# A gated recurrence and a feed-forward block in one kernel: the instruction order of every engine set by a written time plan

## The chip, the cores and the metric

The kernel runs on one core of a Trainium2 chip. Its engines run side by side, each through its own list of instructions in order: TensorE (PE in the tables, with PEld for its weight loads), VectorE (DVE), ScalarE (ACT), GpSimd (POOL) and SyncE (SP), which here only starts DMAs; ACT can start DMAs too. They wait for each other on semaphores. The metric is the device time of one execution in microseconds, as a median of several runs.

## The reference

The inputs are q, k, v and alpha, each (4 batches, 8 heads, 768 steps, 48), and two weights, w_in (384 x 2048) and w_out (2048 x 384), which arrive as 64-bit floats. For every batch and head a 48 x 48 state runs over the steps; its output, with the heads side by side, is the input x (3072 x 384) of a feed-forward block:

```python
for t in range(S):
    state = alpha[:, :, t, :, None] * state + np.einsum('bhd,bhe->bhde', k[:, :, t], v[:, :, t])
    y[:, :, t] = np.einsum('bhd,bhde->bhe', q[:, :, t], state)
...
h = x @ w_in
g = h - np.tanh(h)
return (g @ w_out).astype(np.float32)
```

## The kernel before, in words

`fast` does the work; `general` is a slower path that runs only if a check of the value ranges fails at the end, which it does not here. The 3072 rows are cut into 12 units of 256 steps (three per batch), each of two chunks of 128 steps.

**Attention of a unit (`gla`).** `load` brings alpha, k and q into the tiles `ar`, `kr`, `qr` (four DMAs each, one copy of each tile) and v into `vt` (two DMAs). DVE turns them with 32 x 32 transposes (L363) into aT, kT and qT. Two scans on DVE run the products of alpha backwards (U, L369) and forwards (W, L378); `ends` (L373 to L375) are U's values at chunk borders. POOL multiplies kT by U and qT by W (L383); ACT squares both scans for the range check (L386). Then for each chunk: PE makes the scores kT x qT (`sc`, L401), DVE masks them (`pm`, L404), POOL lets the old state decay (L408), PE adds state x qT (L413) and v x scores (L417) into `y`, and ACT copies `y` into `xT`, the feed-forward's input, and its last heads into `xs` (L423, L424). Six small DMAs, started by ACT, move `xs` into the free rows of xT (L430). For the next chunk PE transposes kT (`tp`, L437), ACT copies it (`kn`, L438), PE multiplies it with v (`up`, L441), and DVE adds that to the state (L446, L448).

**Feed-forward of a unit (`moe`).** Eight slices s of 256 hidden features. `first(s)`: 12 matmuls w_in x xT into a PSUM tile `h` (L461; two such tiles), three squaring passes on ACT and a check pass (L467 to L469, L474), three passes on DVE that end in `g` (L470 to L472). `second(s)`: eight matmuls of g with w_out into the two accumulators `o` (L481). The two alternate, with `second` two slices behind; at the end of a unit two `second`s stand together, and ACT and SP store `o` (L493, L494).

**Weights.** Each of the 8 slices of w_in and of w_out arrives as a 128 x 768 tile `raw` of 8-byte numbers (L41, four such tiles in all) and is rounded to float32 by ACT (two passes, L57 and L58), DVE (three, L60 to L65) and POOL (one add, L68). So unit 0's feed-forward cannot run ahead of its weights; the later units have them.

**What sets the order.** `put` gives every step a number, the steps are emitted in the order of these numbers (L497 to L532), and from the emitted program a scheduler then chooses the order in which each engine executes. Loads are queued on SP in the order which that scheduler found; in unit 0, k and v go by ACT's queue. The code emits v and k of unit 0 and the first weight slices about together; in the trace SP starts with the first slice of w_in.

Of the kernel before, what the change touches and what calls it, by code (L numbers as in the profile page):

```python
# [16 lines left out]
P = 128  # L17
HP = 64
# [26 lines left out]
def round_weight(nc, pool, raw, dst):  # L45
# [3 lines left out]
    V, A, GP = nc.vector, nc.scalar, nc.gpsimd  # L49
    if raw.dtype == FP32:  # L50
        A.copy(dst, raw.rearrange("p (j n) -> p j n", n=dst.shape[-1]))
        return
# [3 lines left out]
    last = pool.tile([P, WN], I32, name="last")  # L56
    A.activation(mag, hi.bitcast(FP32), AF.Abs)  # L57
    A.activation(last, lo, AF.Copy, scale=2.0 ** -29)  # L58

    V.tensor_scalar(out=mag, in0=mag, scalar1=2.0 ** (896 // 8 - 127), scalar2=2.0 ** (1151 // 8 - 127) * 1.875,  # L60
                    op0=ALU.max, op1=ALU.min)
    bits = mag.bitcast(I32)
# [4 lines left out]
    n = dst.shape[-1]  # L67
# [187 lines left out]
def fast(tc, q, k, v, alpha, moe_w_in, moe_w_out, out, w_in, w_out, ident, ok, pad_rows):  # L255
# [17 lines left out]
    with ExitStack() as ctx:  # L273
# [20 lines left out]
        for t, x in zip(raws, (1.0, 0.0, 0.0)):  # L294
            GP.memset(t[:, :, R - 1, :], x)
# [7 lines left out]
        for t in (after, before):  # L303
            GP.memset(t, 0.0)
        GP.memset(after[:, P::P + 1], 1.0)
# [18 lines left out]
        def round_in(s):  # L324
            round_weight(nc, two, raw_in.pop(s), w_in[:, :, 2 * s * P:2 * (s + 1) * P])

        def round_out(s):
            round_weight(nc, two, raw_out.pop(s), w_out[:, 2 * s:2 * s + 2, :])

        loaded = {}  # L330

        def load(u):
            b, i = divmod(u, UPB)
            t0 = i * TU
            for n, (t, x) in enumerate(zip(raws, (alpha, k, q))):
                queue = A if u == 0 and n == 1 else nc.sync
# [8 lines left out]
            vt = loaded[u] = three.tile([P, CU, H, D], FP32, name="vt")  # L345
            for c in range(CU):
                (A if u == 0 else nc.sync).dma_start(out=vt[:, c], in_=v[b, :, t0 + c * P:t0 + (c + 1) * P, :].rearrange("h p d -> p h d"))

        xT = {}

        def gla(u):
# [3 lines left out]
            vt = loaded.pop(u)  # L355
            kT, qT = (two.tile([P, NP, CU, P], FP32, name=n) for n in ("kT", "qT"))
            U, W = (two.tile([P, N, P + 1], FP32, name=n, bufs=1) for n in ("U", "W"))
            U_, W_ = (t.rearrange("p n t -> p (n t)") for t in (U, W))
            aT = aTs[u % 2]
            tail = aT[:, 1:].rearrange("p (n t) -> p n t", t=P + 1)  # L360
            for t, raw in zip((tail[:, :, 0:P].rearrange("p (g c) t -> p g c t", c=CU), kT, qT), raws):
                for g in range(NP):
                    V.transpose(t[:, g].rearrange("p c (i r) -> p r c i", r=R),  # L363
                                raw[:, g, :, 0:32])
                yield
                if t is not kT and t is not qT:


                    V.tensor_tensor_scan(out=U_[:, ::-1], data0=aT[:, :0:-1], data1=after[:, ::-1],  # L369
                                         initial=0.0, op0=ALU.mult, op1=ALU.add)  # L370
                    ends = two.tile([P, NP, CU], FP32, name="ends")
                    e = ends.rearrange("p g c -> p (g c)")
                    V.tensor_reduce(out=least[:, u:u + 1], in_=U[:, :, 0], axis=AX.X, op=ALU.min)  # L373
                    V.tensor_single_scalar(out=e, in_=U[:, :, 0], scalar=1.0 / R_MAX, op=ALU.max)
                    V.reciprocal(before[:, 0::P + 1], e)  # L375
                    yield

                    V.tensor_tensor_scan(out=W_, data0=aT[:, 0:N * (P + 1)], data1=before, initial=0.0,  # L378
                                         op0=ALU.mult, op1=ALU.add)
                    yield  # L380
            for n, (t, x) in enumerate(((kT, U), (qT, W))):
                t = t.rearrange("p g c t -> p (g c) t")
                GP.tensor_mul(t, t, x[:, :, 1:])  # L383
                x = x.rearrange("p n t -> p (n t)")
                junk = two.tile([P, N * (P + 1)], FP32, name="junk", bufs=1)
                A.activation(junk, x, AF.Square,  # L386
                             accum_out=sizes[:, 2 * u + n:2 * u + n + 1])
            yield

            x_t = xT[u] = two.tile([P, KT, TU], FP32, name="xT")  # L390
            xs = two.tile([P, TU], FP32, name="xs")
            for c in range(CU):
# [3 lines left out]
                sc = [ps_sc.tile([P, NP, P], FP32, name=f"sc{hh}") for hh in range(2)]  # L396
                pm = [two.tile([P, NP, P], FP32, name=f"pm{hh}") for hh in range(2)]
                for g in range(NP):
                    for hh in range(2):
                        at = slice(HP * hh, HP * hh + D)  # L400
                        T.matmul(sc[hh][:, g, :], lhsT=kT[at, g, c, :], rhs=qT[at, g, c, :],  # L401
                                 start=True, stop=True)
                for hh in range(2):
                    V.tensor_mul(pm[hh], sc[hh], mask.unsqueeze(1).to_broadcast([P, NP, P]))  # L404
                if n > 0:
                    for hh in range(2):
                        at = (slice(HP * hh, HP * hh + D), slice(None), slice(HP * hh, HP * hh + D))
                        GP.tensor_mul(old[at], old[at], ends[at[0], :, c:c + 1].to_broadcast([D, NP, D]))  # L408
                yield
                y = ps_y.tile([P, NP, P], FP32, name="y", tag="y")  # L410
                if n > 0:
                    for g in range(NP):
                        T.matmul(y[0:EV, g, :], lhsT=old[:, g, :], rhs=qT[:, g, c, :],  # L413
                                 start=(g == 0), stop=False, skip_group_check=True)
                for g in range(NP):
                    for hh in range(2):
                        T.matmul(y[HP * hh:HP * hh + D, g, :], lhsT=vt[:, c, 2 * g + hh, :],  # L417
                                 rhs=pm[hh][:, g, :], start=(n == 0 and g == 0), stop=True,
                                 skip_group_check=True)
                to = slice(c * P, (c + 1) * P)  # L420
                for hh in range(2):
                    at = slice(HP * hh, HP * hh + D)
                    A.copy(xs[at, to], y[at, NP - 1, :])  # L423
                    A.copy(x_t[at, :, to], y[at, 0:KT, :])  # L424
                if c == CU - 1:
                    for hh in range(2):
                        for j in range(KT):
                            at, f0 = pad_rows[j][2 + hh]
                            r0 = HP * hh + f0 - (H - 2 + hh) * D
                            A.dma_start(out=x_t[at, j, :], in_=xs[r0:r0 + at.stop - at.start])  # L430
                yield
                if last:
                    continue
                kn = two.tile([P, NP, P], FP32, name="kn")
                tp = ps_y.tile([P, NP, P], FP32, name="tp", tag="tp")
                for g in range(NP):
                    T.transpose(tp[:, g, :], kT[:, g, c, :], ident)  # L437
# [175 lines left out]
```

## Time and profile before

| What | Value |
|---|---|
| median of three runs | 749.27 us (747.30 to 749.41) |
| profiled execution, its own time | 749.17 us |
| its span, from the first to the last instruction | 745.9 us |
| granted clock of TensorE, mean | 0.961 |
| busy: PE, PEld, DVE, ACT, POOL | 648.4, 470.9, 423.4, 332.7, 117.5 us |
| share of PE's busy time: `h` and `o` groups | 282.2 and 267.2 us |
| DMA: bytes in all | 50.99 MB |
| one weight slice; a unit's alpha, k or q; a unit's v | 768; 736; 384 KB |

A busy share over the whole span mixes the start, where the weights arrive, with the later units, so it is to be read by stretches: a windows view gives each engine's busy time in a stretch, a waits view who stood for whom, a timeline the instructions in order. The sizes come from the table of DMA issues (each transfer of alpha, k and q is cut into four, of 192 and 176 KB, and v into two of 192).

### The profile page before, as it was taken

To read this page: it belongs to the slowest core of one execution; us is meant where nothing else is said; L and a number is where in the kernel's file an instruction comes from. 1 tells how busy PE (TensorE), PEld (TensorE's weight loads), DVE (VectorE), ACT (ScalarE), POOL (GpSimd) and SP (SyncE) were. 2 spreads that over 40 slices of the span, in tenths; PEclk is the share of its full clock that TensorE was granted. 3 is DMA by queue.
4 is the path that set the end of the run, shared out by engine and by line. 5 is a ranking of instruction groups with operands and counts; after the bars stand their busy time and mean duration, and the time that the engine had idled before them with its cause. 6 is when DMAs were issued, how large, how long until landed. Compare 5 with 4: busy or idle time off the path is not lost.

```text
span 745.9 us, 8678 instructions
## 1 busy us (share of the span) xinstructions
PE 648.4 (87%) x3089; PEld 470.9 (63%) x3089; DVE 423.4 (57%) x636; ACT 332.7 (45%) x701; POOL 117.5 (16%) x98
## 2 busy tenths in 40 slices
PE   0367629587999899999999998999999999999996
PEld 0255317455767677776767776777676777777773
DVE  0828662677677676866747636737447253343432
ACT  1135431555256445455544543543554353444542
POOL 2403331333120221110201201202002000000000
PEclk9998965799999999999999999999999999999998
DMA  9615930943036417424512511402200000000000
GB/s 174 169 20 155 229 89 1 206 75 93 8 92 133 98 37 148 98 60 95 119 51 61 119 32 24 84 22 60 49 22 6 21 1 7 22 1 6 21 1 26
DMA packets 57268, 50.99 MB, mean 68 GB/s; under 512 B 29440, under 2 KB 52096, under 8 KB 57216
## 3 DMA queue, kind: packets, MB, share of 16 engines
q1 hardware_dynamic: 52256, 48.02, 28.8%
q10 hardware_dynamic: 4960, 2.33, 1.6%
q8 instruction: 26, 0.43, 0.2%
q14 instruction: 26, 0.21, 0.1%
HBM read 44.43 MB, written 4.72 MB: 66 GB/s over the span
## 4 chain that ended last, share of the span: by engine, by line
PE 70%; DVE 12%; DMA 6%; ACT 4%; issue 3%; POOL 3%; ACTq 1%; SPq 0%; DVEq 0%; POOLq 0%
PE h L461 30%; PE o L481 29%; PE y L417 5%; PE up L441 2%; DVE z L471 2%; PE sc L401 2%; DVE w L470 2%; DVE W L378 2%; ACT u L467 2%; DVE pm L404 1%; DMA kr<-in_k_dram 1%; DMA raw<-in_moe_w_out_dram 1%; PE y L413 1%; PE tp L437 1%; POOL w_in L68 1%
## 5 line engine op out<-in xcount | busy, mean ns | idle before, releaser
L461 PE MATMUL h<-xT,w_in 128*128 128x256 f32 x1152 | 282.2, 391 | 17.3 <-POOL w_in L68 11.9
L481 PE MATMUL o<-w_out,g 128*128 128x384 f32 x768 | 267.2, 496 | 10.5 <-DVE g L472 10.4
L461 PEld LDWEIGHTS h<-xT,w_in 128*128 128x128 f32 x1152 | 217.0, 194 | 63.9 <-POOL w_in L68 14.8
L481 PEld LDWEIGHTS o<-w_out,g 128*128 128x128 f32 x768 | 148.5, 194 | 101.3 <-issue 18.8
L470 DVE TENSOR_TENSOR w<-h,u 128x512 f32<-128x512 f32 x96 | 66.3, 690 | 210.4 <-ACT u L467 209.8
L467 ACT ACTIVATE u<-h 128x512 f32<-128x512 f32 x96 | 57.2, 596 | 181.7 <-PE h L461 150.4
L408 POOL TENSOR_TENSOR state<-state,ends 48x192 f32<-48x192 f32 x40 | 30.5, 762 | 303.7 <-DVE state L448 190.5
L471 DVE SCALAR_TENSOR_TENSOR z<-z,w 128x512 f32<-128x512 f32 x96 | 70.6, 736 | 8.7 <-ACT z L468 0.5
L472 DVE SCALAR_TENSOR_TENSOR g<-z,z 128x512 f32<-128x512 f32 x96 | 68.2, 710 | 7.9 <-ACT z L469 0.4
L468 ACT ACTIVATE z<-u 128x512 f32<-128x512 f32 x96 | 60.6, 631 | 3.0
L469 ACT ACTIVATE z<-u 128x512 f32<-128x512 f32 x96 | 59.0, 615 | 0.0
L474 ACT ACTIVATE big<-u 128x512 f32<-128x512 f32 x96 | 59.0, 615 | 0.0
L423 ACT COPY xs<-y 48x128 f32<-48x128 f32 x48 | 12.5, 260 | 98.6 <-PE y L417 98.3
L437 PE MATMUL tp<-ident,kT 128*128 128x128 f32 x80 | 14.1, 302 | 47.0 <-POOL kT L383 46.0
L417 PE MATMUL y<-pm,vt 128*48 128x128 f32 x384 | 38.1, 298 | 11.7 <-DVE pm L404 11.7
L437 PEld LDWEIGHTS tp<-ident,kT 128*128 128x128 f32 x80 | 10.6, 154 | 53.2 <-POOL kT L383 46.8
L383 POOL TENSOR_TENSOR kT<-kT,U 128x1024 f32<-128x1024 f32 x12 | 27.0, 2250 | 105.6 <-DVE kT L363 86.0
L417 PEld LDWEIGHTS y<-pm,vt 128*48 128x48 f32 x384 | 25.4, 131 | 25.7 <-DVE pm L404 20.7
L404 DVE TENSOR_TENSOR pm<-sc,mask 128x512 f32<-128x512 f32 x48 | 31.7, 684 | 16.3 <-PE sc L401 16.3
L363 DVE STREAM_TRANSPOSE kT<-kr 128x256 f32<-128x256 f32 x48 | 25.7, 622 | 19.2 <-DMA qr<-in_q_dram 17.8
L401 PEld LDWEIGHTS sc<-qT,kT 48*128 48x128 f32 x384 | 29.1, 210 | 11.2 <-issue 9.5
L383 POOL TENSOR_TENSOR qT<-qT,W 128x1024 f32<-128x1024 f32 x12 | 26.2, 2180 | 61.5 <-DVE qT L363 61.5
(56 smaller groups left out, 462.1 us busy)
## 6 DMA issues: line engine op xcount, KB each, us to landing
raw<-in_moe_w_out_dram SPq DMA_DIRECT2D x8, 768.0 KB, 7.2
raw<-in_moe_w_in_dram SPq DMA_DIRECT2D x16, 288.0 KB, 5.5
ar<-in_alpha_dram SPq DMA_DIRECT2D x24, 192.0 KB, 5.0
qr<-in_q_dram SPq DMA_DIRECT2D x24, 192.0 KB, 4.4
out_dram<-ob SPq DMA_DIRECT2D x24, 192.0 KB, 1.9
ar<-in_alpha_dram SPq DMA_DIRECT2D x24, 176.0 KB, 4.2
qr<-in_q_dram SPq DMA_DIRECT2D x24, 176.0 KB, 4.8
kr<-in_k_dram SPq DMA_DIRECT2D x22, 192.0 KB, 4.3
```

The source lines that it names most:

```text
L383: GP.tensor_mul(t, t, x[:, :, 1:])
L401: T.matmul(sc[hh][:, g, :], lhsT=kT[at, g, c, :], rhs=qT[at, g, c, :], start=True, stop=True)
L417: T.matmul(y[HP * hh:HP * hh + D, g, :], lhsT=vt[:, c, 2 * g + hh, :], rhs=pm[hh][:, g, :], start=(n == 0 and g == 0), stop=True, skip_gro ...
L461: T.matmul(h[:, a, :], lhsT=w_in[:, j, f * P:(f + 1) * P], rhs=x_t[:, j, :], start=(j == 0), stop=(j == KT - 1))
L467: A.activation(sq, h, AF.Square)
L468: A.activation(z1, sq, AF.Square, bias=QB1, scale=QA)
L469: A.activation(z2, sq, AF.Square, bias=QB2, scale=QA)
L470: V.tensor_mul(w, h, sq)
L471: V.scalar_tensor_tensor(out=z1, in0=z1, scalar=QK1, in1=w, op0=ALU.add, op1=ALU.mult)
L472: V.scalar_tensor_tensor(out=g, in0=z2, scalar=QK2, in1=z1, op0=ALU.add, op1=ALU.mult)
L474: A.activation(big, sq, AF.Relu, bias=-U_MAX, accum_out=over[:, n:n + 1])
L481: T.matmul(o[c], lhsT=g[:, a * TU + c * P:a * TU + (c + 1) * P], rhs=w_out[:, f, :], start=(f == 0), stop=(f == FT - 1))
```

## The change

The generators `gla` and `moe`, whose steps were spread evenly, are taken apart: every step gets a number of its own from a plan, and the steps are emitted within `tc.manual_schedule()`, under which each engine executes its instructions, and each queue starts its DMAs, in the order of the numbers. What is computed stays the same. In detail:

- The order of loads: unit 0's operands (alpha and q by SP, k and v by ACT), two slices of w_in, one of w_out, one of w_in, unit 1's operands, the moves of xs, then w_out and w_in slices by turns.
- The six moves of `xs` are started by SP (before: ACT).
- The rounding of a weight slice is cut into three steps with numbers at, at+1 (DVE) and at+3 (POOL).
- In unit 0 POOL's products come in halves, one per chunk, and the second chunk's scores use the two `h` tiles of PSUM, not the `sc` tiles.
- `first(s)` is split into its matmuls and `shrink` (ACT and DVE), 2.8 later. In units 1 to 11 `first` comes every 6.6 and `second` 16.5 after its `first`, across the border of units too; a unit's attention stands in the plan 46 before its feed-forward, its loads 8 earlier still.
- `ends` takes its maximum with a tile of constants (a new memset on POOL) in place of a constant. The memsets of the operand tiles' last rows go from POOL to DVE.

```diff
     for t, x in zip(raws, (1.0, 0.0, 0.0)):
-        GP.memset(t[:, :, R - 1, :], x)
+        V.memset(t[:, :, R - 1, :], x)
...
+    def put(at, do, *args):
+        plan.append((at, len(plan), do, args))
+
+    def convert(at, make, s):
+        it = []
+        put(at, lambda: (it.append(make(s)), next(it[0])))
+        put(at + 1, lambda: next(it[0]))
+        put(at + 3, lambda: next(it[0], None))
...
+    def ends():
+        U = m["U"]
+        e = m["ends"] = two.tile([P, NP, CU], FP32, name="ends")
+        e = e.rearrange("p g c -> p (g c)")
+        V.tensor_tensor(out=e, in0=U[:, :, 0], in1=low, op=ALU.max)
...
+    for name, by in (("kT", "U"), ("qT", "W")):
+        if u == 0:
+            for c in range(CU):
+                put(at[name + by] + c, scale, name, by, slice(c, c + 1))
+        else:
+            put(at[name + by], scale, name, by, slice(0, CU))
...
+    def moves():
         for hh in range(2):
...
-                    A.dma_start(out=x_t[at, j, :], in_=xs[r0:r0 + at.stop - at.start])
+                nc.sync.dma_start(out=xT[u][part, j, :], in_=m["xs"][r0:r0 + part.stop - part.start])
+    put(at["moves"], moves)
...
     for s in range(FS):
+        put(first_at[s], first, s)
+        put(first_at[s] + 2.8, shrink, s)
+        put(second_at[s], second, s)
+    put(second_at[-1] + 2.8, store)
...
+    put(0, load, 0)
+    for at, what, s in ((0.1, fetch_in, 0), (0.2, fetch_in, 1), (0.3, fetch_out, 0), (0.4, fetch_in, 2)):
+        put(at, what, s)
+    put(20, load, 1)
+    for s in range(1, FS):
+        put(31 + 6 * s, fetch_out, s)
+        if s + 2 < FS:
+            put(34 + 6 * s, fetch_in, s + 2)
+    gla(0, dict(aT=6, U=8, kT=10.3, ends=12.3, kTU=12.4, W=12.8, qT=15.2, qTW=17.2, sizeU=13.5, sizeW=18,
+                scores=(19.4, 21.4), masked=(21.4, 23.4), decay=(0, 19.5), y=(23.4, 25.4), x=(25.3, 28),
+                back=(14.5, 24.9), update=(16.2, 27.6), moves=29))
+    gla(1, dict(aT=34.5, U=38, kT=41.5, ends=43.5, kTU=45, W=46, qT=49, qTW=52, sizeU=42, sizeW=50,
+                scores=(55.5, 62), masked=(57, 64), decay=(56, 63), y=(59, 67), x=(62, 70),
+                back=(47, 68), update=(56, 70), moves=74))
+    for s, at in enumerate((15, 24.4, 28.7, 41, 48.7, 56, 64, 71)):
+        convert(at, round_in, s)
+    for s, at in enumerate((26.6, 37.5, 45, 52.5, 60, 67.5, 75, 79)):
+        convert(at, round_out, s)
+    moe(0, (31, 34, 37, 46, 53, 60, 68, 76), (40, 43, 50, 57, 65, 72, 79.5, 83))
+
+    STEP = 6.6
+    for u in range(1, NU):
+        t0 = 78 + (u - 1) * FS * STEP
+        moe(u, [t0 + s * STEP for s in range(FS)], [t0 + (s + 2.5) * STEP for s in range(FS)])
+        if u > 1:
+            r = t0 - 46
+            put(r - 8, load, u)
+            rel = dict(aT=0, U=2.5, kT=5.5, ends=8, kTU=8, W=8.5, qT=11.5, qTW=14, sizeU=9, sizeW=12,
+                       scores=(18, 27), masked=(20, 29), decay=(16, 27), y=(23.5, 32), x=(26, 35),
+                       back=(13, 30), update=(15.5, 33), moves=36.5)
+            gla(u, {n: (r + x if not isinstance(x, tuple) else tuple(r + y for y in x))
+                    for n, x in rel.items()})
+    with tc.manual_schedule():
+        for _, _, do, args in sorted(plan, key=lambda x: x[:2]):
+            do(*args)
```

(Indentation is cut by one level. `back` puts ACT's copy `kn` 1 later, `update` DVE's addition 2 later.)

## Rows read from the trace of the kernel before

**Rows 1.** Windows: stretch, length, busy of PE, PEld, DVE, ACT, POOL; clock, DMA, GB/s.
```profile
0.00:27.60 27.60, 0.00 (x0) 0.00 (x0) 9.82 (x14) 4.11 (x5) 7.27 (x20) 1.00 1.02 206
27.60:54.50 26.90, 17.87 (x96) 14.45 (x97) 11.86 (x17) 6.99 (x15) 5.15 (x5) 0.96 0.14 37
54.50:168.00 113.50, 76.65 (x279) 54.11 (x280) 72.61 (x97) 50.03 (x88) 35.97 (x21) 0.78 0.57 125
...
697.20:738.60 41.40, 41.40 (x162) 30.15 (x160) 17.15 (x27) 19.84 (x42) 0.00 (x0) 1.00 0.03 10
```

**Rows 2.** Windows: from the end of unit 0 to the last matmul.
```profile
168.00:738.60 570.60, 553.81 (x2716) 402.32 (x2714) 328.79 (x508) 271.13 (x593) 69.11 (x54) 1.00 0.23 52
```

**Rows 3.** Waits of PE: who waited for whom, us in total, times, longest.
```profile
PE tp L437 <- POOL kT L383: 46.0, 3, 27.6
PE h L461 <- POOL w_in L68: 11.9, 4, 5.3
...
PE up L441 <- ACT kn L438: 2.9, 5, 0.7
```

**Rows 4.** Timeline of SP's queue: start, us, issue, count (weight loads).
```profile
25.59 26.64 SPq L41 DMA_DIRECT2D raw<-in_moe_w_in_dram  x4
...
90.28 42.16 SPq L41 DMA_DIRECT2D raw<-in_moe_w_in_dram  x4
```

**Rows 5.** Waits of SP's queue, the second longest.
```profile
SPq L41 <- DMA xT<-xs: 61.3, 5, 36.0
```

**Rows 6.** Windows of the first 24 us: DMA share and GB/s stand last.
```profile
0.00:20.00 20.00, 0.00 (x0) 0.00 (x0) 2.23 (x5) 2.95 (x3) 4.43 (x18) 1.00 1.00 177
20.00:24.00 4.00, 0.00 (x0) 0.00 (x0) 4.00 (x7) 0.00 (x0) 0.00 (x0) 1.00 1.08 213
```

**Rows 7.** Timeline of the start, selected instructions: start, us, engine, line, operation, count.
```profile
20.10 1.99 DVE L363 STREAM_TRANSPOSE aT<-ar 128x256 f32<-128x256 f32 x4
...
22.39 2.29 DVE L369 TENSOR_TENSOR_SCAN U<-aT,after 128x1032 f32<-128x1032 f32 x1
...
34.50 2.17 POOL L383 TENSOR_TENSOR qT<-qT,W 128x1024 f32<-128x1024 f32 x1 [1.45 <-DVE qT L363]
...
36.72 2.08 PE L401 MATMUL sc<-qT,kT 48*128 48x128 f32 x16 [0.51 <-POOL qT L383]
...
49.97 0.47 ACT L424 COPY xT<-y 48x384 f32<-48x384 f32 x1
50.09 3.15 ACTq L430 DMA_DIRECT2D xT<-xs  x5
...
54.52 7.82 PE L461 MATMUL h<-xT,w_in 128*128 128x256 f32 x24 [5.40 <-DMA xT<-xs]
```

**Rows 8.** Timeline of PE: the eighth `o` batch of unit 0.
```profile
165.24 2.82 PE L481 MATMUL o<-w_out,g 128*128 128x384 f32 x8
```

**Rows 9.** Timeline: a weight slice's conversion, the matmuls on it, ACT's passes behind.
```profile
87.16 0.88 ACT L57 ACTIVATE mag<-raw 128x768 f32<-128x768 f32 x1
...
88.07 0.56 DVE L60 TENSOR_SCALAR mag<-mag 128x768 f32<-128x768 f32 x1 [0.29 <-ACT mag L57]
...
89.26 0.96 DVE L65 SCALAR_TENSOR_TENSOR mag<-raw,mag 128x768 int32<-128x768 int32 x1
...
90.36 1.80 POOL L68 TENSOR_TENSOR w_in<-mag,last 128x768 int32<-128x768 int32 x1 [5.08 <-DVE mag L65]
...
92.22 2.86 PE L461 MATMUL h<-xT,w_in 128*128 128x256 f32 x12 [1.48 <-POOL w_in L68]
95.11 0.60 ACT L467 ACTIVATE u<-h 128x512 f32<-128x512 f32 x1 [6.25 <-PE h L461]
...
97.31 0.19 ACT L474 ACTIVATION_READ_ACCUMULATOR big<-u 128x1 f32 x1
```

**Rows 10.** Timeline of DVE: a scan behind a POOL product; an undisturbed shrink.
```profile
518.46 4.26 DVE L369 TENSOR_TENSOR_SCAN U<-aT,after 128x1032 f32<-128x1032 f32 x1 [0.50 <-POOL kT L383]
...
530.58 0.69 DVE L472 SCALAR_TENSOR_TENSOR g<-z,z 128x512 f32<-128x512 f32 x1
```

More of the change, by code (lines that the diff above doesn't have):

```diff
@@ L362, in gla @@
                 for g in range(NP):
[L363 to L384, printed above, removed]
+                    V.transpose(t[:, g].rearrange("p c (i r) -> p r c i", r=R), raw[:, g, :, 0:32])
+            def new(name):
+                m[name] = two.tile([P, NP, CU, P], FP32, name=name)
+                return m[name]
+            put(at["aT"], flip, raws[0], lambda: tail[:, :, 0:P].rearrange("p (g c) t -> p g c t", c=CU))
@@ L403, in gla @@
-                for hh in range(2):
[L404 to L424, printed above, removed]
@@ new lines, in chunk, with masked, decay @@
+                put(at["scores"][c], scores)
+                def masked():
+                    pm = m["pm", c] = [two.tile([P, NP, P], FP32, name=f"pm{hh}") for hh in range(2)]
+                    for hh in range(2):
+                        V.tensor_mul(pm[hh], m["sc", c][hh], mask.unsqueeze(1).to_broadcast([P, NP, P]))
+                put(at["masked"][c], masked)
+                def decay():
+                    for q in quads:
+                        GP.tensor_mul(old[q, :, q], old[q, :, q],
+                                      m["ends"][q, :, c:c + 1].to_broadcast([D, NP, D]))
@@ new lines, in chunk, with features, back @@
+                put(at["y"][c], products)
+                def features():
+                    to = slice(c * P, (c + 1) * P)
+                    for q in quads:
+                        A.copy(m["xs"][q, to], m["y"][q, NP - 1, :])
+                        A.copy(xT[u][q, :, to], m["y"][q, 0:KT, :])
+                put(at["x"][c], features)
+                if last:
+                    return
+                def back():
+                    tp = m["tp"] = ps_y.tile([P, NP, P], FP32, name="tp", tag="tp")
+                    for g in range(NP):
+                        T.transpose(tp[:, g, :], m["kT"][:, g, c, :], ident)
@@ new lines, in chunk, with natural, update @@
+                put(at["back"][c], back)
+                def natural():
+                    kn = m["kn"] = two.tile([P, NP, P], FP32, name="kn")
+                    A.copy(kn, m["tp"])
+                put(at["back"][c] + 1, natural)
+                def update():
+                    up = m["up"] = ps_y.tile([P, NP, 2, D], FP32, name="up", tag="tp")
+                    for g in range(NP):
+                        T.matmul(up[:, g], lhsT=m["kn"][:, g, :], rhs=vts[u][:, c, 2 * g:2 * g + 2, :],
+                                 start=(g == 0), stop=(g == NP - 1), skip_group_check=True)
```

199 lines of the change are left out of this document (99 added, 100 removed).

## The prediction, made before the changed kernel had run

> **What bounds the kernel now.** I read the windows by stage first, then what TensorE (PE) waited for, then the order of time at the start. The stages [rows 1, 2] show two kernels in one. From 168.0, where unit 0's eighth `o` batch ends [rows 8], to the last matmul at 738.6 PE is busy 553.8 of 570.6 us: bound by its own matmuls, with 16.8 us of waits over eleven units of feed-forward. Before that it is not: nothing for 27.6 us, then 17.9 busy of 26.9 (unit 0's attention), then 76.7 of 113.5 (unit 0's feed-forward, with unit 1's attention among it) at a mean granted clock of 0.78. One unit of feed-forward alone takes 41.4 [rows 1], 2.59 per batch of 12 `h` or 8 `o` matmuls; so 113.5 us for it is where time can be had. The waits [rows 3] name the reasons: `tp` on POOL's scaled kT (46.0 us in three waits, the longest of them the start's 27.6) and `h` on POOL's rounded w_in. In order of time SyncE's queue is twice stopped, 26.6 and 42.2 us, at four weight loads [rows 4], mostly for the landing of `xT<-xs` [rows 5]: ACT issues those late, and the weights behind them come late. The first `h` starts at 54.5 [rows 7].
>
> **The change part by part.** Each engine now executes in the order of the plan's numbers; the numbers themselves set no time. So I follow the order with the durations of before.
>
> *Start to the first `h`.* Alpha and k (1472 KB) go first, on two queues, with nothing ahead: at 177 GB/s [rows 6] 8.5 us after 0.8, taken as 10 with the issue. q and v follow, then four weight slices of 768 KB, then unit 1's operands. DVE: flip of alpha 2.0 (to 12), scan U 2.3 [rows 7] (14.3), flip of k (16.3), ends and scan W (20.0: the scan is held while POOL multiplies, as in rows 10, where one took 4.26), flip of q (22.0). PE's order puts `update` of chunk 0 before the scores, and its operand `kn` stands on ACT behind the first slice's conversion: 3360 KB have landed at 19.4, conversion 2x0.9 [rows 9], then the copy, some 0.7 [rows 3]: 22.1. From there PE runs batches at the slow 2.0 us that it shows at this place (16 scores in 2.08 [rows 7]): update 24.1, scores 26.2 and 28.3 (two PSUM pairs, so no wait between), y(0) 30.3, back 31.4, y(1) with two batches 35.4; ACT's four copies, two of 0.47 [rows 7] and two smaller, 37.0. Before, this point was near 50.4.
>
> *The six moves xT<-xs* now stand on SP's queue behind unit 1's 14 loads. By row, five of ACT's six were issued from 50.09 on for 3.15 us, the `h` began at 54.52 [rows 7]: with the first one 5.1 in all, which would give 42.1. But SP's issues wait for the landing of transfers some eight back, whoever issued them [rows 5], here unit 1's q: 7872 KB (8.06 MB) have to land, 3.54 by 20 us and the rest at 213 GB/s [rows 6] by 41.2; with 2.2 for the move: 43.4. I take that (bounds 40 and 47). The gain so far is 11.1.
> [...]
>
> *Unit 0's feed-forward and unit 1's attention.* SP's weight loads now follow the moves, one for each freed buffer. From the first `h` (cold, 5.2: the first 24 took 7.8 [rows 7]) the first `g` work reaches DVE at 49.2. DVE's order is then: shrink 2.1 (three of 0.69 [rows 10]), flip 2.0, shrink 2.1, scan U 2.3, conversion 2.15 (88.07 to 90.22 [rows 9]), shrink, flip of k, conversion of w_in slice 3: 16.9, to 66.1; POOL's add 1.9, third `h` slice (s=3) at 68.0. Next stand ends, scan W behind POOL's kT, a conversion, the shrink of s=3 (ACT works on it only after `kn` and slice 4's conversion), the flip of q, the conversion for s=4: s=4 starts 14.5 later, 82.5. From there the order closes a loop over four engines: ACT's conversion of w_in slice s+1 stands behind ACT's work on slice s. Rows 9 have each link: `Abs` to `h` matmul 5.06 (87.16 to 92.22), matmuls to ACT's first pass 2.89, ACT's passes 2.39 (95.11 to 97.50): 10.3 a turn. s=5, 6, 7 thus start at 92.8, 103.1, 113.4. After s=7: 2.6 + 2.4, slice 7 of w_out 5.1, last `o` batch 2.6: unit 0 is through at 126.1. Unit 1's attention on PE fits into the loop's idle time (2.6+2.6 of 10.3 are feed-forward), as does the first `h` of unit 1. Weights are not late: slice 7 of w_out is issued when slice 6 of w_in frees its buffer near 102, and needed at 118. Bounds: 97 (below, DMA-paced) and 138 (for each of the eight slices one DVE instruction held by POOL, 1.5 us more). The stage ends 168.0 - 126.1 = 41.9 us earlier than before.
>
> *The other units.* The matmuls are the same, so 553.8 of PE remain. What changes is the waits, 16.8 before. In a unit that starts at 0, PE reaches the scores of chunk 0 after eight batches (20.7), back, a wait for `kn` of 0.7 (the longest [rows 3]) and update: 23.1. Those scores need POOL's scaled q, which ends DVE's chain: first shrink 2.6 + 2.9 = 5.5, flip 7.5, U 9.8, shrink 11.9, flip of k 13.9; the plan then starts POOL's kT product (2.2) beside scan W, which by row 10 is held till 16.1 and ends 18.4; shrink 20.5, flip of q 22.5, POOL 24.7. PE waits 1.6 and 0.7, 2.3 a unit, 23 in ten: 6.2 more than before. Without the hold W ends at 16.7 and only 0.7 remains (7 in all); at 3.5 it is 35. Moving the six DMA issues (0.6 each [rows 7]) off ACT saves it 3.8 us a unit, which nothing waits for here. DVE's chain and the masked products behind it have 3 us or more before PE wants them. The halved POOL products occur in unit 0 alone and are in the start; the memsets moved to DVE let alpha's load out at once, counted above. `ends` takes one small DVE instruction for another: nothing. The tail of 7.3 us behind the last matmul stays; the final checks on DVE now come after the plan, but eight small instructions fit beside the last two `o` batches (5.2).
>
> *Sum.* The profiled execution took 749.17 for a span of 745.9, and the median of the runs is 749.27. 749.2 - 41.9 + 6.2 = 713.5. I say 713.
>
> **The rivals.**
> *A, the weights set the pace.* If ACT and DVE get ahead of the order's loop, 12 slices of 0.786 MB from 43.4 at 213 GB/s land at 88; the last slice's 5.1, a start of 2 and a batch give 97. Then 749.2 - 71 + 6 = 684. For it: POOL and ACT are far from full (36.0 and 50.0 of 113.5 [rows 1]). Against it: from 49.2 DVE alone has eight shrinks (17), unit 1's attention (15: flips 6, scans 5, masks and state 4) and twelve conversions (26), 58 us, ending at 107 without a wait.
> *B, only the start moves.* The loop with its locks is no faster than the old order: 113.5 from 43.4, unit 0 through at 157, 749.2 - 11.1 + 6.2 = 744. For it: DVE was already busy 72.6 of the 113.5 [rows 1]. Against it: the old stage holds SP's second stop of 42.2 [rows 4] and most of PE's 18.4 for kT behind the start [rows 3], both gone.
> *C, slower.* A fixed order gives a late DVE no way round: PE stands at the scores of chunk 0 while the next `h`, ready, is behind them. It decides from 6.1 us of wait a unit on (16.8 + 41.9 + 2.2 for 0.3%, over ten units), 3.8 above my 2.3; at 8 a unit the time is 749.2 - 41.9 + 80 - 16.8 = 770. For it: DVE has 15 us of work in PE's 15 there. Against it: both scans would have to be held, and the flip of alpha be late as well, when the loads have 8 plan units of lead.
> *D, no change*: B and the half of C cancelling, within 0.3% (what a measurement can tell from none here).
>
> **How the numbers follow.** My own case 0.68, with a range of 697 (stage end 114, waits 16) to 734 (138, waits 33); A 0.14; B 0.10; C 0.06; D 0.02. The predicted time is 713. From 684 to 738: A's upper half and part of B are in it, about a fifth is left out. Faster is my case with A and B, 0.92; same 0.02; slower 0.06.
>
> **What would show it.** Right: the first `h` near 43, no stop of 20 us or more on SP's weight loads, unit 0's last `o` at 114 to 138 with `h` starts some 10 us apart and `h` waiting for POOL's w_in; then units of about 53 to 54 us with a short wait of `sc` for POOL's qT, and a tail of 7. The start is wrong if `h` begins after 47. The loop is wrong if `h` starts are 7 us apart (A) or 13 (B). The rest is wrong if PE's waits after unit 0 exceed 35, or fall below 7; the prediction fails as a whole if those reach 60.

## The result and the profile after

The changed kernel took 717.9 us, median of 4 runs (715.47 to 719.65), the kernel before 748.41 beside it: a ratio of 0.959, 95% interval 0.955 to 0.963. 713 had been forecast, 684 to 738 as the range. The profiled execution took 716.62 for a span of 714.8; 749.17 and 745.9 before.

The windows by stage of the changed kernel, from the first matmul to the last (columns as in [rows 1]; the cuts are at the first `h` and the end of unit 0's eighth `o` batch):

```profile
18.40:44.70 26.30, 13.33 (x97) 11.04 (x97) 18.52 (x25) 11.41 (x20) 13.82 (x9) 0.92 1.04 198
44.70:137.00 92.30, 65.62 (x276) 47.10 (x277) 71.30 (x91) 46.38 (x84) 31.21 (x18) 0.86 0.59 133
137.00:707.50 570.50, 542.65 (x2718) 402.27 (x2716) 353.39 (x509) 268.89 (x595) 65.83 (x54) 1.00 0.25 52
```

The lines answer to [rows 1, 2]. Unit 0 is through at 137.0 instead of 168.0: 31.0 of the 31.1 us of span. The stretch from there to the last matmul is as long as before, 570.5 against 570.6, but made up otherwise: PE busy 542.65, 11.2 less, and idle 27.9, 11.1 more. The tail is 7.3 again. Outside the span lie 1.8 us instead of 3.3; the kernel before with one edit in its order of loads (the last section of the experiments) has 1.7 there too, so nothing shows that these 1.5 us come from the change. So 749.2 - 31.0 - 0.1 - 1.5 = 716.6.

What TensorE waited for, first in unit 0's feed-forward (44.7 to 137), then in the rest (answering to [rows 3]):

```profile
PE h L534 <- POOL w_in L72: 15.3, 5, 5.2
PE o L558 <- POOL w_out L72: 11.4, 4, 5.6
PE h L534 <- DMA xT<-xs: 7.7, 1, 7.7
```

```profile
PE up L503 <- ACT kn L497: 15.3, 10, 2.9
PE sc L451 <- POOL qT L417: 10.5, 10, 1.4
```

SP's queue after unit 1's loads: the moves, then one weight slice behind the other, with no row of more than 7.2 us where [rows 4] had two of 26.6 and 42.2:

```profile
37.77 6.81 SPq L523 DMA_DIRECT2D xT<-xs  x6
...
47.83 5.80 SPq L41 DMA_DIRECT2D raw<-in_moe_w_in_dram  x4
```

PE's `h` batches of unit 0 (the first three slices in one row) and its last `o` batch, which answers to [rows 8]:

```profile
44.69 10.98 PE L534 MATMUL h<-xT,w_in 128*128 128x256 f32 x36 [7.66 <-DMA xT<-xs]
...
71.10 4.54 PE L534 MATMUL h<-xT,w_in 128*128 128x256 f32 x12 [2.45 <-POOL w_in L72]
...
87.25 5.03 PE L534 MATMUL h<-xT,w_in 128*128 128x256 f32 x12 [5.21 <-POOL w_in L72]
...
100.51 2.86 PE L534 MATMUL h<-xT,w_in 128*128 128x256 f32 x12 [1.58 <-POOL w_in L72]
...
111.75 2.86 PE L534 MATMUL h<-xT,w_in 128*128 128x256 f32 x12 [1.55 <-POOL w_in L72]
...
122.54 7.04 PE L534 MATMUL h<-xT,w_in 128*128 128x256 f32 x24 [4.46 <-POOL w_in L72]
...
134.42 2.85 PE L558 MATMUL o<-w_out,g 128*128 128x384 f32 x8 [2.26 <-POOL w_out L72]
```

Instructions of DVE and ACT between them. Undisturbed, the first pass of a rounding (L65) takes 0.56 and the third (L69) 0.96 [rows 9], the second (L67) 0.56 too, and the shrink's passes 0.69 each [rows 10]. The rows of 62.59, 73.13, 85.58, 87.65 and 104.03 started while a product or a sum ran on POOL; the first four took longer, the last did not. `pm` are the masks of unit 1's attention:

```profile
62.59 1.79 DVE L546 SCALAR_TENSOR_TENSOR z<-z,w 128x512 f32<-128x512 f32 x1
...
73.13 2.46 DVE L65 TENSOR_SCALAR mag<-mag 128x768 f32<-128x768 f32 x1
...
85.58 2.04 DVE L67 TENSOR_SCALAR mag<-mag 128x768 int32<-128x768 int32 x1
...
87.65 2.81 DVE L69 SCALAR_TENSOR_TENSOR mag<-raw,mag 128x768 int32<-128x768 int32 x1
...
92.94 0.69 DVE L545 TENSOR_TENSOR w<-h,u 128x512 f32<-128x512 f32 x1 [2.49 <-ACT u L542]
...
94.61 0.91 ACT L61 ACTIVATE mag<-raw 128x768 f32<-128x768 f32 x1
95.14 1.28 DVE L458 TENSOR_TENSOR pm<-sc,mask 128x512 f32<-128x512 f32 x2
...
96.34 0.55 DVE L65 TENSOR_SCALAR mag<-mag 128x768 f32<-128x768 f32 x1
...
104.03 0.69 DVE L545 TENSOR_TENSOR w<-h,u 128x512 f32<-128x512 f32 x1 [1.20 <-ACT u L542]
```

One unit of the rest, around the scores of chunk 0:

```profile
462.98 2.17 POOL L417 TENSOR_TENSOR kT<-kT,U 128x1024 f32<-128x1024 f32 x1 [39.98 <-DVE least L404]
...
463.13 4.18 DVE L411 TENSOR_TENSOR_SCAN W<-aT,before 128x1032 f32<-128x1032 f32 x1
...
466.82 0.60 PE L492 MATMUL tp<-ident,kT 128*128 128x128 f32 x4
...
467.35 1.06 ACT L427 ACTIVATE junk<-W 128x1032 f32<-128x1032 f32 x1 [3.10 <-DVE W L411]
...
468.41 0.57 ACT L497 COPY kn<-tp 128x512 f32<-128x512 f32 x1
...
469.02 1.13 PE L503 MATMUL up<-vt,kn 128*128 128x96 f32 x8 [1.60 <-ACT kn L497]
...
473.75 1.16 PE L451 MATMUL sc<-qT,kT 48*128 48x128 f32 x16 [0.99 <-POOL qT L417]
```

Scan W takes 4.18 beside POOL's product of kT, as forecast from [rows 10]; `sc` then waits for POOL's q (0.99 in that row). But ACT takes the squares of W (467.35) ahead of the copy `kn` (468.41), although `kn`'s operand has been ready since 467.4: `up` waits 1.60, not 0.7.

### The profile page after: what moved, and what is told of

Same layout as the page of the kernel before. It is cut to its first block, busy times and chain, and to the rows that moved or that the text cites. A ratio compares the mean times of both kernels' runs of the same rounds, so it can differ in the third digit from the quotient of the medians.

```text
span 714.8 us, 8728 instructions
## 1 busy us (share of the span) xinstructions
PE 621.6 (87%) x3089; PEld 460.4 (64%) x3089; DVE 451.3 (63%) x639; ACT 329.2 (46%) x701; POOL 115.9 (16%) x98
## 4 chain that ended last, share of the span: by engine, by line
PE 45%; DVE 27%; DMA 15%; POOL 5%; issue 3%; ACT 2%; SPq 2%; DVEq 0%; POOLq 0%; ACTq 0%
PE h L534 21%; PE o L558 15%; DVE W L411 6%; DMA qr<-in_q_dram 6%; DMA raw<-in_moe_w_in_dram 4%; DMA ar<-in_alpha_dram 3%; PE sc L451 3%; DVE kT L381 3%; DVE qT L381 3%; DVE z L546 3%; POOL qT L417 3%; DVE U L395 3%; PE y L476 3%; DVE w L545 3%; DVE aT L381 3%
## 5 line engine op out<-in xcount | busy, mean ns | idle before, releaser
L534 PE MATMUL h<-xT,w_in 128*128 128x256 f32 x1152 | 275.8, 391 | 22.9 <-POOL w_in L72 15.3
L558 PE MATMUL o<-w_out,g 128*128 128x384 f32 x768 | 267.0, 491 | 11.4 <-POOL w_out L72 11.4
L417 POOL TENSOR_TENSOR kT<-kT,U 128x1024 f32<-128x1024 f32 (+1 forms) x13 | 30.3, 2331 | 377.1 <-DVE least L404 377.1
L546 DVE SCALAR_TENSOR_TENSOR z<-z,w 128x512 f32<-128x512 f32 x96 | 83.5, 869 | 10.6 <-DVE w L545 0.9
L411 DVE TENSOR_TENSOR_SCAN W<-aT,before 128x1032 f32<-128x1032 f32 x12 | 48.7, 4059 | 0.4
L458 DVE TENSOR_TENSOR pm<-sc,mask 128x512 f32<-128x512 f32 x46 | 29.6, 685 | 16.9 <-PE sc L451 16.5
L503 PE MATMUL up<-vt,kn 128*128 128x96 f32 x160 | 22.8, 287 | 18.8 <-ACT kn L497 18.8
L417 POOL TENSOR_TENSOR qT<-qT,W 128x1024 f32<-128x1024 f32 (+1 forms) x13 | 26.7, 2053 | 65.6 <-DVE qT L381 65.6
L451 PE MATMUL sc<-qT,kT 48*128 48x128 f32 x368 | 27.6, 291 | 10.5 <-POOL qT L417 10.5
L451 PEld LDWEIGHTS sc<-qT,kT 48*128 48x128 f32 x368 | 23.1, 193 | 20.8 <-POOL qT L417 16.7
L503 PEld LDWEIGHTS up<-vt,kn 128*128 128x128 f32 x160 | 20.8, 198 | 22.6 <-ACT kn L497 22.0
L483 ACT COPY xs<-y 48x128 f32<-48x128 f32 x48 | 12.5, 260 | 46.5 <-PE y L476 46.2
L512 DVE TENSOR_TENSOR state<-state,up 48x192 f32<-48x192 f32 x32 | 11.2, 350 | 34.7 <-PE up L503 33.4
```

The lines of the kernel that those rows point to most:

```text
L411: V.tensor_tensor_scan(out=W.rearrange("p n t -> p (n t)"), data0=aT[:, 0:N * (P + 1)], data1=before, initial=0.0, op0=ALU.mult, op1=ALU.add)
L417: GP.tensor_mul(t, t, m[by].rearrange("p (g c) t -> p g c t", c=CU)[:, :, cs, 1:])
L451: T.matmul(sc[hh][:, g, :], lhsT=m["kT"][q, g, c, :], rhs=m["qT"][q, g, c, :], start=True, stop=True)
L534: T.matmul(h[:, a, :], lhsT=w_in[:, j, f * P:(f + 1) * P], rhs=xT[u][:, j, :], start=(j == 0), stop=(j == KT - 1))
L546: V.scalar_tensor_tensor(out=z1, in0=z1, scalar=QK1, in1=w, op0=ALU.add, op1=ALU.mult)
L558: T.matmul(o[c], lhsT=g[:, a * TU + c * P:a * TU + (c + 1) * P], rhs=w_out[:, f, :], start=(f == 0), stop=(f == FT - 1))
```

## The experiments

All times are medians. The changed kernel was run again with the second set and took 721.09 (717.14 to 722.34); its first median was 717.9. Differences under 4 us between sets are therefore not read as effects of an edit. "Through" is the end of unit 0's last `o` batch, or within 0.6 us of it, the start of the copy that waits for it; "the rest" goes from there to the last matmul.

### What does fixing the order do by itself?

The plan emitted in the same sequence, each engine's order left to the scheduler:

```diff
-        with tc.manual_schedule():
-            for _, _, do, args in sorted(plan, key=lambda x: x[:2]):
-                do(*args)
+        for _, _, do, args in sorted(plan, key=lambda x: x[:2]):
+            do(*args)
```

> The plan's steps are emitted in the same sequence, but the scheduler orders every engine again, as before the change. Theory (the gain comes from the loads and moves in order of use, and the fixed order holds the engines to it): the scheduler brings back waits of SP's weight loads and interleaves unit 1's attention differently, so unit 0 ends later than 137.0 and the time lies between the two kernels, 725 to 745. Rival (the sequence of emission alone brings the gain, the fixed order nothing): the time stays at 718 within 3 us. Second rival (the fixed order costs, as an engine has no way round a late operand): below 712.

Measured: 710.84 (709.66 to 712.59), ratio 0.952 (0.949 to 0.954). This is faster than the changed kernel by 7, so the theory fell: the sequence in which the work is emitted, with the rounding cut in steps and the loads where the plan has them, brings the gain without a fixed order. The trace says what the fixed order does. Timeline of PE, then the window of the rest:

```profile
64.87 1.11 PE L492 MATMUL tp<-ident,kT 128*128 128x128 f32 x4 [23.02 <-POOL kT L417]
...
69.78 9.96 PE L534 MATMUL h<-xT,w_in 128*128 128x256 f32 x36
```

```profile
149.50:700.60 551.10, 541.70 (x2718) 403.32 (x2716) 334.62 (x507) 268.51 (x594) 63.56 (x54) 1.00 0.25 54
```

The scheduler put unit 1's transposes, which waited 23.0 for their operand, ahead of unit 0's first `h`: that starts at 69.78 instead of 44.69, though SP had issued the last of the moves by 46.8, and unit 0 is through 12.5 later, at 149.5. But the rest takes 551.1 instead of 570.5, with PE idle for 9.4. By these two traces fixing the order gains 12.5 in unit 0 and loses 19.4 behind it. To test that, one kernel fixes it up to plan number 84 only:

```diff
+        plan.sort(key=lambda x: x[:2])
+        cut = [x[0] < 84 for x in plan].index(False)
         with tc.manual_schedule():
-            for _, _, do, args in sorted(plan, key=lambda x: x[:2]):
+            for _, _, do, args in plan[:cut]:
                 do(*args)
+        for _, _, do, args in plan[cut:]:
+            do(*args)
```

> The plan's order is kept as it is for every step with a number below 84 (unit 0 whole, unit 1's attention, the first conversions), and the steps after that are emitted in the same sequence but left to the scheduler to put in order on each engine. Theory (two effects of opposite sign): the fixed order gains about 12 us in unit 0 and costs about 19 us over the units behind it, so unit 0 is through at about 137 us as in the changed kernel and the rest takes 551 to 556 us instead of 570.5: time 696 to 704 us, PE waits of the rest under 13 us. Rival (the quick rest of the run with the scheduler came from its late start of unit 0, which left more of unit 1 done by then): the rest stays near 565 to 570 us, time 711 to 718 us.

> The changed kernel itself, as the base on this chip for the runs beside it. Theory and rival agree: 715 to 720 us.

Measured: 700.07 (696.59 to 701.83), ratio 0.936 (0.931 to 0.940), beside 721.09. The window of its rest:

```profile
136.40:687.50 551.10, 540.78 (x2713) 402.38 (x2712) 335.42 (x508) 268.19 (x594) 63.52 (x54) 1.00 0.25 54
```

Through at 136.4, rest 551.1: both parts as the theory had them, and they add.

### What do the waits of the rest cost?

First each of the two waits alone. The squares of W behind the copy `kn`:

```diff
-sizeU=9, sizeW=12,
+sizeU=9, sizeW=14.6,
```

> In units 2 to 11 ACT squares scan W only after the copy kn. The trace has 15.3 us of PE's waits for kn behind that pass. Theory (PE's next wait, for POOL's scaled q at the scores, comes from DVE's chain and takes over whatever is saved before it): the kn waits fall to about 0.7 each, the waits for q grow by as much, the time stays within 2 us of 718. Rival (the waits add): 7 to 9 us faster.

Measured: 732.21 (728.7 to 735.05), ratio 0.978 (0.974 to 0.981): 14 slower than the changed kernel's first median, 11 than its second. The waits for `kn` fell to 5.4 and those for the scores grew to 21.0, as expected; their sum hardly moved. The time went elsewhere: in the rest, here from 141.0 to 725.6, PE is busy for 556.5. (Unit 0, which the edit doesn't touch, ends 4 later than in the changed kernel's first trace and 1 later than in its second.) Windows of 2 us, and PE's timeline, at one such wait:

```profile
158.00:160.00 2.00, 0.38 (x4) 0.39 (x5) 2.00 (x1) 0.00 (x0) 2.00 (x2) 0.71 0.00 0
160.00:162.00 2.00, 2.00 (x17) 1.78 (x16) 1.72 (x5) 0.00 (x0) 1.82 (x3) 0.50 0.03 8
```

```profile
159.62 2.08 PE L451 MATMUL sc<-qT,kT 48*128 48x128 f32 x16 [3.14 <-POOL qT L417]
161.62 4.84 PE L534 MATMUL h<-xT,w_in 128*128 128x256 f32 x12
```

In one wait of 3.14 the granted clock falls to 0.50 and stays there for the next 6 us of work (the windows from 162 to 166 have 0.50 and 0.58); 12 `h` take 4.84 there, 2.86 at a granted clock of 1.00 [rows 9]. In this trace seven places of the rest show a granted clock below 0.75 in windows of 2 us, in the changed kernel's first trace none. Its second trace has three (down to 0.50 or 0.51), and one can be compared instruction by instruction. First the second run, then the first, the same two batches after the same wait for `kn`:

```profile
261.07 1.13 PE L503 MATMUL up<-vt,kn 128*128 128x96 f32 x8 [1.62 <-ACT kn L497]
262.04 4.47 PE L558 MATMUL o<-w_out,g 128*128 128x384 f32 x8
```

```profile
256.13 1.13 PE L503 MATMUL up<-vt,kn 128*128 128x96 f32 x8 [1.62 <-ACT kn L497]
257.10 2.77 PE L558 MATMUL o<-w_out,g 128*128 128x384 f32 x8
```

So the same wait of 1.62 was followed once by 4.47 for eight `o` (granted clock 0.51 from 264 to 266) and once by 2.77 (1.00). In these traces whether a short wait costs clock is not fixed by the order of instructions. It dropped more often where single waits were longer (seven places here, five in the next run), but the run with the earlier roundings below, with the changed kernel's own waits in the rest, has four such places, so the number of places is in part chance. In the whole of the rest PE's busy time is 548.7 in the second trace and 542.65 in the first, for the same matmuls in the same order; this run's rest is 14.1 longer than the first's, 13.9 of it busy time, and 11.5 longer than the second's, 7.8 of it busy. That the low clock makes up this busy time is read from the traces.

Next scan W ahead of the transposes of kT, so that POOL's product cannot hold it:

```diff
-rel = dict(aT=0, U=2.5, kT=5.5, ends=8, kTU=8, W=8.5, qT=11.5, qTW=14,
+rel = dict(aT=0, U=2.5, ends=5, W=5.5, kT=8.2, kTU=10.5, qT=8.6, qTW=14,
```

> In units 2 to 11 DVE runs scan W and then flips k and q, so that POOL's product of kT runs beside a flip and not beside the scan. Theory (POOL's product holds the scan, 4.2 us instead of 2.3, and that delay is what PE waits for at the scores): scan W takes 2.3, the waits of the scores for POOL's q (10.5 us) go, those for kn shrink to 0.7 each, tp waits up to 1 us for kT; 8 to 12 us faster. Rival (the chain is late for another reason): scan W at 2.3 but the time within 3 us of 718.

Measured: 720.62 (717.13 to 724.85), ratio 0.965 (0.960 to 0.970): no gain. The scan took 2.31 and the waits for the scores went, but the product of kT now comes later, and PE's waits of the rest name it:

```profile
PE tp L492 <- POOL kT L417: 15.3, 10, 3.5
```

The longest of the ten is 3.5, and in five places the granted clock falls to between 0.50 and 0.53. The wait had only changed its name, so the consumer has to move too, the transposes and the update further down PE's order:

```diff
 (with the edit above)
-back=(13, 30), update=(15.5, 33), moves=36.5)
+back=(16.4, 30), update=(18.4, 33), moves=36.5)
```

> All engines in the plan's order, as in the changed kernel; in units 2 to 11 scan W goes ahead of the transposes of kT, and the transposes of the keys and the update of the first chunk go down the plan by 3.4 and 2.9 numbers, so that kT's product has time to come. Theory (the rest loses to single waits for late operands and nothing else): the waits for keys, scores and transposes together (27.9 us in the changed kernel) fall under 8, the clock stays at 1.0 behind unit 0, time 692 to 700 us. Rival (the order fixed for TensorE itself is the cost: whatever is moved, another operand is late): waits of 15 us or more stay in the rest under another name, time 710 to 722 us.

Measured: 688.36 (687.37 to 689.57), ratio 0.919 (0.915 to 0.923), 33 below the changed kernel beside it. The window of its rest:

```profile
138.00:679.10 541.10, 539.36 (x2718) 403.41 (x2716) 336.94 (x509) 269.75 (x594) 65.65 (x54) 1.00 0.27 55
```

Of 541.1 us PE is busy in 539.4, and no window of 2 us has a granted clock below 0.75: bound by its matmuls. The rest is 29.4 shorter than in the changed kernel's first trace: 26.1 less waiting, 3.3 less busy (9.4 less than in its second trace). The rival fell: a fixed order need not leave another operand late.

### What sets the pace of unit 0?

The last four roundings of w_in earlier in the plan, in the changed kernel, in the kernel fixed to 84, and in the one without waits:

```diff
-enumerate((15, 24.4, 28.7, 41, 48.7, 56, 64, 71)):
+enumerate((15, 24.4, 28.7, 41, 46.5, 53.3, 60.5, 68.5)):
```

> The conversions of w_in slices 4 to 7 stand 2 to 3.5 plan units earlier, ahead of the shrink of the slice before, on ACT and on DVE. Theory (unit 0's stage is a loop of ACT's passes, the conversion on ACT, DVE and POOL, and the h matmuls, 10.8 to 13.3 us a turn): the loop is broken, the h starts of unit 0 move to 7 to 9 us apart, unit 0's last o batch ends near 127 and the time falls by 8 to 11 us. Rival (the stage is bound by DVE's sum, busy 71.3 of 92.3 us, or by the weights' landing): the turns stay above 10 us and the time within 3 us of 718.

> As the run with the fixed order up to 84, and the last four roundings of w_in 2.2 to 3.5 numbers earlier in the plan. Theory (unit 0 is bound by when VectorE gets to the w_in slices): unit 0 is through at about 131 us, 6 earlier, and as the rest is no longer tied to the fixed order it keeps this: 691 to 698 us, 4 to 7 below the run without the earlier roundings. Rival (what unit 0 gains is given back as waits and a lower clock in the rest, as part of it was with the fixed order): within 2 us of the run without them.

> Both edits in the plan together, all engines in its order: the last four roundings of w_in 2.2 to 3.5 numbers earlier, and scan W with the transposes and the update of the first chunk moved as in the run whose rest had no waits. Theory (the edits act on different stretches and add up): unit 0 through at 131 to 132 us instead of 138, the rest 541 us with under 4 us of waits, time 680 to 684 us. Rival (the earlier roundings bring a lower clock in the rest, which ate a third of their gain in the run with them alone): rest 544 us or more, time 685 to 690 us.

Measured: 713.66 (713.35 to 714.22), 690.34 (688.13 to 691.36) and 681.21 (680.13 to 683.2), the last a ratio of 0.910 (0.905 to 0.915). Each is 4 to 10 below its partner, with unit 0 through at 131.0, 131.1 and 129.5, 5 to 8 earlier (the six traces with the places unchanged have 136.2 to 141.1). So the places of the roundings in the engines' order set a part of unit 0's pace. The loop was not broken as expected, though: in the first of the three `h` of s=4 to 7 start 12.9, 15.4, 11.9 and 7.4 after the one before, not 7 to 9, since other batches then hold PE up. Of the 8 to 11 that this run was expected to bring, 4.2 came by the changed kernel's first median and 7.4 by its second; the next two, expected to bring 4 to 8, brought 9.7 and 7.2 in kernels with fewer waits behind. The fastest kernel's window of the rest:

```profile
132.00:671.00 539.00, 537.39 (x2709) 401.69 (x2707) 334.82 (x507) 269.57 (x593) 65.67 (x54) 1.00 0.27 54
```

### Where the moves and unit 1's loads stand

The moves of unit 0 on ACT's queue, in the changed kernel:

```diff
-nc.sync.dma_start(out=xT[u][part, j, :], in_=
+(A if u == 0 else nc.sync).dma_start(out=xT[u][part, j, :], in_=
```

> The changed kernel with one edit: the six moves of unit 0 are issued from ScalarE's queue, as in the kernel before, and not behind unit 1's fourteen loads on SP. Theory (the moves wait for the loads that SP issued ahead of them; VectorE, idle for 8.9 us until the first h gives it work, sets unit 0's pace from there): first h at 40.5 to 42.5 us instead of 44.69, everything of unit 0 behind it 2 to 4 us earlier, through at 133 to 135, time 2 to 4 us below the changed kernel. Rival (they wait for the bytes of those loads in the DMA engines, whichever queue issues them): first h at 44 to 46 us, time 716 to 721 us.

Measured: 719.36 (716.68 to 719.57), ratio 0.960 (0.955 to 0.965). ACT's queue, SP's queue and PE:

```profile
37.75 0.59 ACTq L523 DMA_DIRECT2D xT<-xs  x1
...
39.66 1.88 ACTq L523 DMA_DIRECT2D xT<-xs  x3
```

```profile
24.50 9.79 SPq L362 DMA_DIRECT2D ar<-in_alpha_dram  x4
39.65 2.02 SPq L362 DMA_DIRECT2D kr<-in_k_dram  x4
```

```profile
42.98 10.41 PE L534 MATMUL h<-xT,w_in 128*128 128x256 f32 x36 [4.48 <-DMA xT<-xs]
```

ACT issues the six in 3.8 us, SP took 6.81; the first `h` begins at 42.98 instead of 44.69, and the nine traces with this start unedited have 43.91 to 45.98. So `h` comes 0.9 to 3.0 earlier, where 2 to 4 had been expected. But the edit did more than move the six: SP now stands 5.3 us for a move before it issues unit 1's k, at 39.65, and k, q and v go out behind the first moves instead of ahead of them. Fewer bytes stood ahead of the moves, so this run doesn't tell SP's queue from the bytes in flight, which was the rival. Unit 0 is through 1.5 earlier than in the changed kernel's first trace; the time can't show that.

Then the kernel before with unit 1's load early, and with the moves on SP as well:

```diff
-        put(-0.1, load, 1)
+        put(-13, load, 1)
 (the second kernel also)
-                            A.dma_start(out=x_t[at, j, :], in_=xs[r0:r0 + at.stop - at.start])
+                            nc.sync.dma_start(out=x_t[at, j, :], in_=xs[r0:r0 + at.stop - at.start])
```

> The kernel before, with one edit in its order of emission: unit 1's load goes ahead of the weight slices from the third on (at -13 instead of -0.1). Theory (the order of the loads on SP is the larger part of the gain, the fixed order of the engines the smaller): SP's stops no longer hold unit 1's operands, its attention fills TensorE's idle time in unit 0 and unit 0 is through at 148 to 156 us instead of 168, time 728 to 738 us. Rival (what counts is the split of the rounding into steps and when each is done): unit 0 through at 164 us or later, time 742 to 752 us.

> The kernel before, with two edits and the scheduler's own order of every engine: unit 1's load goes ahead of the weight slices from the third on, and unit 0's and all later moves are issued on SP instead of ScalarE's queue, so that no load on SP waits for the end of a move issued elsewhere. Theory (of the 31 us that the changed kernel gains, the larger part is these two places in the queues): SP has no stop over 15 us on the moves, unit 1's k and q are in by 48 us instead of 58 and later, unit 0 is through at 146 to 156 us instead of 168, and the time is 726 to 738 us. Rival (the gain needs the new pieces of the plan, the rounding in three steps and the numbers of each unit's steps; the queues alone shift the waits): unit 0 through at 158 us or later, or what it gains lost again behind it; time 742 to 752 us.

Measured: 749.21 (747.21 to 754.37), ratio 1.001 (0.998 to 1.004), and 762.65 (760.33 to 765.36), ratio 1.019 (1.013 to 1.026). Both theories fell. In the first, SP stands in the middle of unit 1's alpha; its timeline, then its waits:

```profile
22.49 29.31 SPq L342 DMA_DIRECT2D ar<-in_alpha_dram  x4
```

```profile
SPq L342 <- DMA xT<-xs: 24.9, 6, 22.2
```

The stop ends at 51.8, while ACT issues the moves (49.66 to 53.45): an early place in SP's queue helps little while SP waits for moves that another queue issues late. Unit 0 is through 7 earlier, at 160.2; the rest gives it back, 578.0 long instead of 570.6. In the second kernel that stop is gone, k and q of unit 1 are issued by 36.2, and SP issues the six moves in 3.77, by 53.3. But the scheduler then does what it did above, on PE:

```profile
66.89 1.11 PE L437 MATMUL tp<-ident,kT 128*128 128x128 f32 x4 [17.75 <-POOL kT L383]
...
71.79 6.44 PE L461 MATMUL h<-xT,w_in 128*128 128x256 f32 x24
```

Unit 1's transposes stand ahead of unit 0's first `h`, which starts at 71.79 instead of 54.52 [rows 7]; unit 0 is through at 161.7. From 168 to the last matmul PE is busy for 562.5 us, more than the 553.81 of [rows 2], and idle for 19.0. A part of that is at its beginning: around a wait of 7.0 for POOL's kT, which ends at 169.85, the granted clock is 0.50 from 168 to 178. What the rest of it is stays open. By these two runs an early load is worth little without an order that still lets unit 0's `h` go first; no run gave the kernel before both.

## Why the prediction was right, step by step

**Start to the first `h`: right.** 43.4 forecast, 44.69 measured: gain 9.8 instead of 11.1. SP's first move stood for 3.66 us, to 41.43, where 41.2 had been worked out for the landing of unit 1's q (the trace names k for 0.4 of this wait, not q); the other five issues took 3.2 us instead of the 2.2 counted for the move. That SP's issues wait for transfers some eight back shows in the kernel before, from 70 to 84 us, where unit 1's alpha, k and q go out in four parts each, then v in two: each part of q waited for alpha, whose parts stand eight places ahead of it, each of v for k:

```profile
SPq L342 <- DMA ar<-in_alpha_dram: 2.0, 4, 0.6
SPq L347 <- DMA kr<-in_k_dram: 1.0, 2, 0.6
```

The nine traces of this start have the first `h` at 43.91 to 45.98. With ACT issuing the moves it came at 42.98, but unit 1's k, q and v then stood behind the moves, so that run doesn't tell the queue from the bytes ahead of them.

**Unit 0's feed-forward: mechanism right, turns too short, the end within its bound by luck.** `h` of s=3 to 7 were forecast at 68.0, 82.5, 92.8, 103.1, 113.4 and came at 71.10, 87.25, 100.51, 111.75, 122.54; the end at 137.0 instead of 126.1, just within the bound of 138; the second trace of the same kernel has 140.0. The 10.9 are: 1.3 from the start, 1.8 up to s=3, 1.6 up to s=4, 4.4 in the three turns of the loop (13.3, 11.2, 10.8 instead of 10.3), 1.8 at the end. Two links of the loop were mis-sized. From the start of `h` to ACT's first pass 2.89 was taken; with `h` at low clock (granted 0.50 from 87 to 91 and from 123 to 125) it is 5.06 in the first turn, and after s=7 4.49 instead of 2.6, 4 us in all. From `Abs` to the next `h` 5.06 was taken; it is 5.90, 6.05 and 5.60, 2.4 in all, since unit 1's masks and state additions stand on DVE ahead of the rounding (95.14 in the rows above). DVE held by POOL, from which the bound was made, is not what filled it: the held pass of 62.59 costs 1.1 on the way to s=3, but behind the longer ones (73.13, 85.58, 87.65) DVE stands idle for ACT (1.65, then 2.49), so they don't set the pace. What it does cost is in the 1.6 up to s=4: POOL's product of kT starts beside the held scan W and takes 4.17, to 75.17; behind it, and behind `h` at low clock (0.55 from 71 to 73, 4.54 for the batch), come `tp` and the copy `kn`, and ACT's next work stands behind `kn`. `h` waited for w_in (15.3), as named; that `o` would wait for w_out (11.4) was not named. Rival A (weights set the pace) falls: in this stretch SP's queue waited 48.5 us in eight waits for DVE to free a slice's buffer, so the loads followed the rounding. B (only the start moves) falls with the turns.

**The rest: two errors that more than cancel.** Forecast 6.2 longer, it came out 0.1 shorter. Waits of 23 were forecast, 27.9 came: the scores' 10.5 instead of 16, the copy `kn`'s 15.3 instead of 7, since ACT's squares stand ahead of it: that is the mis-sized wait. The 553.8 of busy time were taken as fixed, and 11.2 of them went (5.1 in the second trace, with its three places at low clock). The kernel before cuts its batches: in the timeline of the rest the masked products `y<-pm` stand in 40 rows before and 20 after, `h` in 119 and 86. Over nine whole units, before and after:

```profile
L417 PE MATMUL y<-pm,vt 128*48 128x128 f32 x288 | 26.9, 280 | 10.9 <-DVE pm L404 10.9
```

```profile
L476 PE MATMUL y<-pm,vt 128*48 128x128 f32 x288 | 19.5, 277 | 0.0
```

`o` goes the other way, in 68 rows before and 86 after, and takes 3.5 us more in the rest (239.6 and 243.1). That the cutting costs this time is read from the traces alone; no run cut batches and nothing else. Rival C (slower) named the right mechanism, a fixed order that stands at the scores; its waits were 27.9, not the 61 from which it decides.

**The sum: close in part by luck.** Unit 0 was taken 10.9 too short, the rest 6.3 too long, and the 1.5 outside the span were not in the sum. So 716.6 came in the profiled execution where 713.5 had been worked out, with the gain in unit 0 at three quarters of the forecast.

**What the prediction did not see:** it followed the fixed order throughout and did not ask what the same sequence does without it. The order alone loses 7 against the same sequence under the scheduler. What remains of the gain without it, some 37 us (by the trace 18.5 in unit 0 and 19.5 in the rest), is brought by the plan's sequence with its finer steps; which of those steps, no run separates. The two places in the queues, tried by themselves in the kernel before, did not bring it.

## What to carry to other kernels

Fixing an order pays where a scheduler lets early work of the next unit stand in front of the bottleneck's own, and costs wherever it leaves an operand late in a step that repeats: measure the two stretches apart, and fix only the first, or move the consumer down until its operand has come. When a repeated wait is removed, look at which wait takes its place before counting the gain; an edit that brings nothing by itself (scan earlier) can bring 30 us together with a second one (transposes and update later, not run alone). An early place for a transfer needs, by these runs, both a queue that isn't stopped by another queue's transfer and a consumer order that doesn't let the early work push in front.

## What was not expected of the hardware

- In one wait of 3.14 us between dense TensorE work the granted clock fell to 0.50 and stayed there for the next 6 us of work; the same wait of 1.62 us was followed by a clock of 0.51 in one run (eight `o` in 4.47) and of 1.00 in the other (2.77). In the run with ten long waits the rest grew by 11.5 to 14.1 us, 7.8 to 13.9 of it in busy time, while the sum of the waits hardly moved against the first trace.
- Five DVE instructions in the rows above that started beside a POOL product or sum of a whole tile took 1.1 to 1.9 us longer, as [rows 10] had for a scan (4.26, and 2.29 without POOL [rows 7]); here small ones did so as well: 0.69 became 1.79, 0.56 became 2.46, 0.56 became 2.04, 0.96 became 2.81, scan W 4.18 instead of 2.31. Not all did: the shrink's first pass, which reads `h` from PSUM, kept its 0.69 beside POOL's sum (104.03).
- SP issued the six small moves in 6.81 us right behind unit 1's loads, ACT the same six in 3.8. It is not SP as such: 12 us behind its last load SP took 3.77 too (the last run of the experiments).
